# Window attention and two MLPs on one core: dilated rows in 1 KB runs, and a new order for the start

## The chip, the core and the metric

The kernel runs on one core of one Trainium2 chip. The core has five engines that run side by side, each with an instruction queue that it works through strictly in order: TensorE (PE, matmuls and transposes into PSUM), VectorE (DVE), ScalarE (ACT), GpSimd (POOL) and SyncE (SP, which here only issues DMAs). An instruction waits on semaphores until its inputs are there, and whatever stands behind it on the same engine waits with it. The metric is device time in microseconds. Before the change, three runs took 951.55, 952.68 and 952.71 us (median 952.68).

## The reference

Three stages in a row, all in float32:

```
attention   q, k, v of 4 batches x 8 heads x 576 positions x 64
            heads 0-3: each position sees itself and the 31 before it
            heads 4-7: itself and 31 more, every 4th position back (dilation 4)
            softmax over those, times v
x           the attention output as 2304 tokens x 512
MLP 1       h = x @ w_in1 (512 x 2048);  g = max(0.01 h, h);   y = g @ w_out1
MLP 2       h = y @ w_in2;  g = max(h,0) + log1p(exp(-|h|));   out = g @ w_out2
```

The weights come as 64-bit floats. They are read as pairs of 32-bit words and put together on the chip.

## The kernel before

**Stages.** The 2304 tokens are cut into eight blocks (`w` = 0 to 7) of 288, half a batch each. A block's attention is done in four pairs of heads (`p` = 0 to 3; pairs 0 and 1 are plain, 2 and 3 dilated). Below, pairs 0 to 3 are those of block 0 and pairs 4 to 7 those of block 1. MLP 1 runs in slots: for one block and one of 16 chunks of 128 hidden units, `g1` (12 matmuls on L586, 128x128 by 288 columns) makes the hidden values in PSUM, ACT and DVE split them into a high and a low half (`gh`, `gl`), and `g2` (12 matmuls on L620) adds to the output two slots later. Each product is done three times, high by high, high by low, low by high, so that fp32r matmuls give float32 precision. Slots 0 to 3 are block 0 with weight chunks 0 to 3, slots 4 to 7 block 1 with the same chunks, slots 8 to 11 block 0 with chunks 4 to 7, and so on. MLP 2 follows in blocks of 384 tokens. From about 130 us on TensorE is fed without a break, so the order of work matters in the start alone.

**The early blocks.** Blocks 0 and 1 (`early`) have their own way through attention. `load_rows` loads the rows of q or k of four heads (one plain or one dilated group) into a tile `rows`; `pe_trans` (L402) transposes them on TensorE, two heads at a time; `evac_k`, `evac_q` (L417, L420) copy them from PSUM to SBUF on ACT; `scores_early` (L451 the mask, L455 the products) makes the scores; `scores_copy` copies one half of them to SBUF on ACT (L469) and one on DVE (L471); `rowmax` (L506) takes the maximum on POOL; `less_max` (L510, DVE) and `exp` (L513, ACT) follow; `pv` (L526), `inv` (L536 to L538, DVE), `xT` (L549), `x_hi` (L562, ACT) and `x_lo` (L566, DVE) make the block's x in two halves. The first `g1` of a block needs all four pairs.

The dilated rows are loaded so that token 4p+i stands in partition p, place i, with the four heads side by side. A run of consecutive bytes is then one token of one head, 64 numbers or 256 B, and one DMA is issued for each i:

```
t = wraw.tile([n // nb, nb, 4, D], F32, tag="raw", name="rows", bufs=NRAW)
rs = src[self.b, self.h0:self.h0 + 4, lo:self.s0 + T1, :].rearrange("h (p i) d -> i p h d", i=nb)
for i in range(nb):
    eng.dma_start(out=t[:, i], in_=rs[i])
```

Block 0's q rows are issued by ACT, all other DMAs by SP.

**Weights.** Each of 32 pieces of MLP 1 (piece 2f for chunk f of w_in, 2f+1 for w_out) is loaded (L221, L225) and converted in a chain: ACT `cf` (L232), DVE `cp` (L236), DVE join (L240), ACT low word (L245), add (L249), ACT high half `w` (L269), low half (L274). The add and the low half of pieces 0 to 5 run on DVE, those of pieces 6 to 21 on POOL. POOL holds one library at a time: the maxima need one, the adds and low halves another, and the adds wait (`order=early`) until all eight maxima of blocks 0 and 1 are done, so that the library is changed once there. The first piece on POOL, number 6, is the w_in of chunk 3, which slot 3 needs.

**Late blocks.** Blocks 2 to 7 use other buffers (`kt`, `qz`, `v`), which POOL clears once in the start (`late_clear`, L317).

**The order.** Nothing is in a fixed order: every step is an `Op` with an engine, an assumed cost, what it depends on and a due time. `run_schedule` plays the program through with those costs, lets each engine take the ready step that is due first, and emits the instructions in that order. `COLD` multiplies the assumed TensorE costs of block 0, `lag` is the assumed time from an issued DMA to its use, `TL` the due time of the clears, `TR` that of block 1's maxima relative to slot 0. A changed cost can so reorder every engine.

Of the kernel before, what the change touches and what calls it, by code (L numbers as in the profile page):

```python
# [22 lines left out]
def kernel(  # L23
# [75 lines left out]
    def run_schedule(slots):  # L99
# [226 lines left out]
    class Pair:  # L326
# [25 lines left out]
        def load_rows(self, which, eng):  # L352
# [4 lines left out]
            t = wraw.tile([n // nb, nb, 4, D], F32, tag="raw", name="rows", bufs=NRAW)  # L357
            rs = src[self.b, self.h0:self.h0 + 4, lo:self.s0 + T1, :].rearrange("h (p i) d -> i p h d", i=nb)
            for i in range(nb):
                eng.dma_start(out=t[:, i], in_=rs[i])  # L360
# [35 lines left out]
        def pe_trans(self, which):  # L396
            src = rows[self.w, self.dil, which]
            pp, nb = src.shape[0], src.shape[1]
            o = 2 * (self.p % 2)
            ps = ps_y.tile([P, nb, pp], F32, tag=f"y{o + which}", name="tr")  # L400
            for i in range(nb):
                nc.tensor.transpose(  # L402
                    out=ps[:, i], in_=src[:, i, o:o + 2, :].rearrange("p h d -> p (h d)"), identity=ident[0:pp, 0:pp])
# [62 lines left out]
        def scores_copy(self, j):  # L466
            o = self.s[:, :, j]
            if j == 0:
                nc.scalar.activation(out=o, in_=self.sc[j], func=AF.Copy)  # L469
            else:  # L470
                nc.vector.tensor_copy(out=o, in_=self.sc[j])  # L471
# [275 lines left out]
    COLD = 1.6  # L747
    TL, TR = 30.0, -12.0
# [29 lines left out]
    for t, to in [(t, 0.0) for t in kt_b + qz_b] + [(t, 1.0) for t in v_b]:  # L778
        late_clear.append(Op("pool", 0.7, clear, nc.gpsimd, t, to, order=late_clear[-1:], target=TL))
    for w in range(NW):  # L780
        first_slot = min(s for s in range(NS1) if order[s][0] == w)
        for p in range(NPAIR):
# [14 lines left out]
            if early:  # L797
                if p % 2 == 0:
                    ls = []
                    for which in (1, 0):  # L800
                        qd = "dma" if which or w else "act"
                        nb = 4 if dil or w and which else 3
                        o = Op(qd, 0.48 * nb, a.load_rows, which, nc.scalar if qd == "act" else nc.sync, acq=["raw"],
# [3 lines left out]
                        ls.append(Op("bw", 1.1 if w == 0 else 1.4, lambda: None, deps=[o], **m))  # L807
                    early_rows[w, dil] = ls
                lk, a.lq = early_rows[w, dil]
            else:  # L810
                lk = Op("dma", 1.95, a.load_k, order=[prev(1, "lq")], acq=["kr"], **m)
                a.lq = Op("dma", 1.95, a.load_q, order=[lk], acq=["qr"], **m)
# [256 lines left out]
```

## Time and profile before

| | us |
|---|---|
| median of three runs | 952.68 |
| the profiled execution, whole time | 952.19 |
| its span, first to last instruction | 950.3 |
| TensorE busy | 926.1 (97% of the span) |
| VectorE busy | 665.2 (70%) |
| ScalarE busy | 469.4 (49%) |
| GpSimd busy | 162.6 (17%) |

1.9 us of the profiled execution lie outside its span. The shares are means over the whole; the change touches the first 100 us, and there each stretch has another limit. Of the last chain, 89% of the span is TensorE and 6% VectorE, and the VectorE part lies almost wholly before 130 us.

### The profile page before, as it was taken

Reading aid. Unit: us, or ns where it says so; the run is one execution under the profiler, and the core shown is the slowest. Engines: PE = TensorE matmul, PEld = TensorE weight load, DVE = VectorE, ACT = ScalarE, POOL = GpSimd, SP = SyncE. Lnnn points to the kernel's source line nnn. Section 1 sums busy time; section 2 is a strip of 40 time slices with the busy share of each in tenths; the row PEclk is TensorE's granted clock in tenths of the full one; section 3 lists DMA queues with packets and bytes.
Section 4 is the critical chain, followed back from the end, with each engine's and each line's share of the span. In section 5 each row is a group of like instructions: output and inputs, shape, how many; then the busy total and the mean of one; then the engine's idle time right before and its main releaser. Section 6 shows DMA issues by size and latency. Waiting matters only on the chain.

```text
span 950.3 us, 15906 instructions
## 1 busy us (share of the span) xinstructions
PE 926.1 (97%) x6002; PEld 876.8 (92%) x6002; DVE 665.2 (70%) x1313; ACT 469.4 (49%) x973; POOL 162.6 (17%) x114
## 2 busy tenths in 40 slices
PE   7989899999999999999999999999999999999997
PEld 6788799999999999999999989899899899899896
DVE  6678899667466674665744487777877877877775
ACT  4566675344344443444446654644644645544543
POOL 4537731011010110200208710000000000000000
PEclk9999899999999999999999999999999999999999
DMA  9968001546264444453257410200200000000000
GB/s 216 256 192 277 10 1 29 142 118 155 93 151 109 142 105 131 123 122 119 76 175 239 136 35 1 66 1 1 67 1 1 34 1 1 34 1 1 34 1 33
DMA packets 137552, 81.52 MB, mean 86 GB/s; under 512 B 101380, under 2 KB 121860, under 8 KB 137476
## 3 DMA queue, kind: packets, MB, share of 16 engines
q1 hardware_dynamic: 135076, 79.92, 29.8%
q10 hardware_dynamic: 2400, 0.59, 0.4%
q8 instruction: 47, 0.77, 0.3%
q14 instruction: 29, 0.24, 0.1%
HBM read 62.65 MB, written 17.83 MB: 85 GB/s over the span
## 4 chain that ended last, share of the span: by engine, by line
PE 89%; DVE 6%; ACT 1%; DMA 1%; issue 1%; POOL 0%; SPq 0%; DVEq 0%; ACTq 0%
PE h L586 40%; PE yo L720 20%; PE yp L620 19%; PE pv L526 4%; PE sc L482 2%; DVE cf L240 2%; DVE cp L236 1%; PE sc L455 1%; PE xt L549 1%; DVE gl L607 1%; DMA rows<-in_k_dram 1%; PE tr L402 1%; PE sc L451 0%; DMA raw<-in_moe_w_out_dram 0%; ACT cf L232 0%
## 5 line engine op out<-in xcount | busy, mean ns | idle before, releaser
L586 PE MATMUL h<-xh,w 128*128 128x288 f32 (+1 forms) x1792 | 447.6, 319 | 1.8 <-POOL w L274 1.8
L586 PEld LDWEIGHTS h<-xh,w 128*128 128x128 f32 x1792 | 316.4, 191 | 6.3 <-POOL w L274 2.1
L586 PE MATMUL h<-xl,w 128*128 128x288 f32 (+1 forms) x896 | 283.7, 317 | 0.1
L620 PE MATMUL yp<-gh,w 128*128 128x288 f32 x1024 | 232.4, 301 | 7.3 <-DVE ys L634 3.6
L620 PEld LDWEIGHTS yp<-gh,w 128*128 128x128 f32 x1024 | 173.5, 189 | 8.9 <-DVE ys L634 4.3
L720 PE MATMUL yo<-w,gh 128*128 128x512 f32 x576 | 180.3, 394 | 0.3 <-ACT gh L703 0.3
L586 PEld LDWEIGHTS h<-xl,w 128*128 128x128 f32 x896 | 170.8, 191 | 4.6 <-DVE xl L566 0.3
L620 PE MATMUL yp<-gl,w 128*128 128x288 f32 x512 | 152.3, 297 | 0.0
L607 DVE TENSOR_TENSOR gl<-hc,gh 128x288 fp32r<-128x288 f32 x128 | 74.0, 578 | 94.5 <-ACT gh L603 93.3
L676 ACT ACTIVATE ex<-h 128x384 f32<-128x384 f32 x96 | 47.2, 491 | 174.5 <-PE h L586 174.5
L720 PEld LDWEIGHTS yo<-w,gh 128*128 128x128 f32 x576 | 106.9, 188 | 18.3 <-ACT gh L703 1.2
L720 PE MATMUL yo<-w,gl 128*128 128x512 f32 x288 | 114.4, 397 | 0.2 <-DVE gl L707 0.2
L603 ACT ACTIVATE gh<-hc 128x288 fp32r<-128x288 f32 x128 | 56.7, 443 | 88.3 <-PE yp L620 87.5
L598 ACT ACTIVATE hc<-h 128x288 f32<-128x288 f32 x128 | 52.2, 408 | 94.7 <-PE h L586 90.9
L506 POOL PARTITION_ALL_REDUCE mx<-s x24 | 48.0, 2001 | 296.2 <-DVE s L496 288.2
L620 PEld LDWEIGHTS yp<-gl,w 128*128 128x128 f32 x512 | 96.9, 189 | 0.0
L687 DVE TENSOR_SCALAR z<-ex 128x384 f32<-128x384 f32 x96 | 35.5, 370 | 77.2 <-ACT ex L677 77.2
L720 PEld LDWEIGHTS yo<-w,gl 128*128 128x128 f32 x288 | 54.1, 188 | 13.7 <-DVE gl L707 1.3
L694 DVE TENSOR_TENSOR ln<-ln,ex 128x384 f32<-128x384 f32 x96 | 54.5, 568 | 3.2
L707 DVE TENSOR_TENSOR gl<-ln,gh 128x384 fp32r<-128x384 f32 x96 | 53.6, 558 | 3.6 <-ACT gh L703 1.6
L696 DVE SCALAR_TENSOR_TENSOR ln<-h,ln 128x384 f32<-128x384 f32 x96 | 53.5, 558 | 3.2
L690 DVE TENSOR_TENSOR z<-ex,z 128x384 f32<-128x384 f32 x96 | 53.6, 558 | 3.0
(73 smaller groups left out, 1062.3 us busy)
## 6 DMA issues: line engine op xcount, KB each, us to landing
raw<-in_moe_w_in_dram SPq DMA_DIRECT2D x32, 512.0 KB
raw<-in_moe_w_out_dram SPq DMA_DIRECT2D x32, 512.0 KB
w<-cf SPq DMA_DIRECT2D x32, 256.0 KB
w<-w SPq DMA_DIRECT2D x32, 256.0 KB
y<-ys SPq DMA_DIRECT2D x8, 576.0 KB
out_dram<-o SPq DMA_DIRECT2D x18, 256.0 KB
qr<-in_q_dram SPq DMA_DIRECT2D x96, 36.0 KB
yr<-y SPq DMA_DIRECT2D x4, 576.0 KB
```

The costliest lines, as they stand in the source:

```text
L506: nc.gpsimd.partition_all_reduce(self.mx, self.sf, channels=P, reduce_op=bass_isa.ReduceOp.max)
L586: nc.tensor.matmul(out=h, lhsT=a[:, c, :], rhs=b_[:, c, :], start=(c == 0 and a is whi and b_ is xh), stop=(c == NC - 1 and a is wlo))
L598: nc.scalar.activation(out=hc, in_=hbank.pop(s), func=AF.Prelu, alpha=0.01)
L603: nc.scalar.activation(out=gh, in_=hcopy[s], func=AF.Copy)
L607: eng.tensor_sub(out=gl, in0=hcopy.pop(s), in1=gparts[s][0].bitcast(F32))
L620: nc.tensor.matmul(out=ybank[e], lhsT=a[:, e * P:(e + 1) * P], rhs=b_, start=(first and a is whi and b_ is gh), stop=(last and a is wlo))
L676: nc.scalar.activation(out=ex, in_=hbank[NS1 + s], func=AF.Abs)
L690: nc.vector.tensor_sub(out=z, in0=ex, in1=z)
L694: nc.vector.tensor_tensor(out=ln, in0=ln, in1=ex, op=ALU.min)
L696: nc.vector.scalar_tensor_tensor(out=ln, in0=hbank.pop(NS1 + s), scalar=0.0, in1=ln, op0=ALU.max, op1=ALU.add)
L707: nc.vector.tensor_sub(out=gl, in0=soft.pop(s)[1], in1=gh.bitcast(F32))
L720: nc.tensor.matmul(out=obank[c, t], lhsT=a[:, t * P:(t + 1) * P], rhs=b_, start=(f == 0 and a is gh and b_ is whi), stop=(f == NF - 1 and ...
```

## The change

Four things. The dilated rows of blocks 0 and 1 are loaded by one DMA each, with the four tokens of a partition in one run of 4 x 64 numbers (1 KB). Two heads no longer stand side by side, so a transpose takes two neighbouring residues (tokens 4p+2u and 4p+2u+1) of one head: the 64-row halves of `kt`, `qt` are then residues, no longer heads, the number of transposes and matmuls is the same, and `scores_copy` puts the pieces back in the old order with a strided output. The transfer time of row loads and other loads is modelled apart from the issue (`landing`), with other costs. Due times change: `COLD` 1.6 to 1.2, `TL` from a due time of 30 to an earliest time of 36, `TR` -12 to -2. And with these the order changes on every engine.

```
         def load_rows(self, which, eng):
...
+            if self.dil:
+                t = wraw.tile([n // nb, 4, nb, D], F32, tag="raw", name="rows", bufs=NRAW)
+                eng.dma_start(
+                    out=t.rearrange("p h i d -> p h (i d)"),
+                    in_=rs.rearrange("h (p i) d -> p h (i d)", i=nb))
+            else:
...
         def pe_trans(self, which):
...
+            if self.dil:
+                cols = [src[:, o + j, 2 * u:2 * u + 2, :] for j in range(2) for u in range(2)]
+            else:
+                cols = [src[:, i, o:o + 2, :] for i in range(src.shape[1])]
...
         def scores_copy(self, j):
-            o = self.s[:, :, j]
+            if self.dil:
+                o = self.s[:, j::2]
+                i = self.sc[j].rearrange("x (h u) m -> x u h m", h=2)
+            else:
+                o, i = self.s[:, :, j], self.sc[j]
...
-                return 2.0
+                return 1.5
...
-    COLD = 1.6
-    TL, TR = 30.0, -12.0
+    COLD = 1.2
+    TL, TR = 36.0, -2.0
...
-        late_clear.append(Op("pool", 0.7, clear, nc.gpsimd, t, to, order=late_clear[-1:], target=TL))
+        late_clear.append(Op("pool", 0.7, clear, nc.gpsimd, t, to, order=late_clear[-1:], start=TL))
...
+    def landing(op, us, m):
+        return Op("bw", us, lambda: None, deps=[op], **m)
...
-                        o = Op(qd, 0.48 * nb, a.load_rows, ...
+                        o = Op(qd, 0.75 if dil else 0.65 * nb, a.load_rows, ...
-                        ls.append(Op("bw", 1.1 if w == 0 else 1.4, lambda: None, deps=[o], **m))
+                        ls.append(landing(o, 1.3 if dil else 0.47 * nb, m))
...
-                lk = Op("dma", 1.95, a.load_k, order=[prev(1, "lq")], acq=["kr"], **m)
-                a.lq = Op("dma", 1.95, a.load_q, order=[lk], acq=["qr"], **m)
+                o = Op("dma", 1.95, a.load_k, order=[prev(1, "i_lq")], acq=["kr"], **m)
+                lk = landing(o, 1.0, m)
+                a.i_lq = Op("dma", 1.95, a.load_q, order=[o], acq=["qr"], **m)
+                a.lq = landing(a.i_lq, 0.9, m)
```

On SP the change takes 3 + 3 + 3 issues away (three dilated loads of four DMAs each become one), on ACT 3. The sixth weight piece, which stood behind block 1's v and dilated rows, now stands right behind the first five, and block 0's dilated v ahead of block 1's dilated rows.

At the very start TensorE had twelve transposes of plain rows, then four of dilated rows, then the scores of pairs 0 and 1, then twelve more dilated transposes. Now the scores of pairs 0 and 1 follow the twelve plain transposes, and all sixteen dilated ones come after them.

The second place is TensorE ahead of the first product of MLP 1 (`h`). In the rows 96 is a plain pair and 72 a dilated one (and `tr` 104 the k rows of a dilated pair of block 1). Before: the second half of `pv` of pair 2, `xt` of pair 1, `pv` of pair 3, `xt` 2, `pv` 4, `xt` 3, `pv` 5, `xt` 4, first `h`:

```order
L526 MATMUL pv<-ev,es 72x65 x4
L549 MATMUL xt<-ident,xn 128x96 x3
L526 MATMUL pv<-ev,es 72x65 x8
L549 MATMUL xt<-ident,xn 128x72 x4
L526 MATMUL pv<-ev,es 96x65 x6
L549 MATMUL xt<-ident,xn 128x72 x4
L526 MATMUL pv<-ev,es 96x65 x6
L549 MATMUL xt<-ident,xn 128x96 x3
L586 MATMUL h<-xh,w_313 128x288
```

Now: the second half of `pv` of pair 3, `xt` 2, a transpose of pair 7's k, `pv` 4, the scores of pair 7 (the mask matmuls and `ekq`), `xt` 3, first `h`:

```order
L543 MATMUL pv<-ev,es 72x65 x4
L566 MATMUL xt<-ident,xn 128x72 x4
L414 MATMUL tr<-ident,rows 128x104 x4
L543 MATMUL pv<-ev,es 96x65 x6
L464 LDWEIGHTS identb
L464 MATMUL sc<-masksb,identb 128x288
L464 LDWEIGHTS identb
L464 MATMUL sc<-masksb,identb 128x288
L468 MATMUL sc<-ekq 128x72 x8
L566 MATMUL xt<-ident,xn 128x72 x4
L603 MATMUL h<-xh,w_378 128x288
```

`pv` 5 and `xt` 4 of block 1 moved behind the first `h`, and the scores of pairs 6 and 7 moved nearer to it.

On DVE the copies of the scores of pairs 6 and 7 (`es_106`, `es_107`) stood early, around the low half of the second w_in chunk:

```order
L566 TENSOR_TENSOR xl_451<-xt_452,xh_450 128x288
L471 COPY es_106<-sc_474 128x288
L274 TENSOR_TENSOR w0_495<-cf_287,w0_495 128x512
L471 COPY es_107<-sc_499 128x288
L236 TENSOR_SCALAR cp_425<-cf_424 128x512
```

Now they stand behind the low half of x of pair 3 (`xl_369<-xt_566`), the last that the first `h` needs:

```order
L583 TENSOR_TENSOR xl_369<-xt_566,xh_368 128x288
L553 TENSOR_SCALAR rd_583<-pv_537 96x6
L554 RECIPROCAL rd_583<-rd_583 96x6
L555 TENSOR_TENSOR xn_536<-pv_537,rd_583 96x384
L527 TENSOR_TENSOR es_105<-es_105,emx_113 128x576
L236 TENSOR_SCALAR cp_562<-cf_561 128x512
L488 COPY es_106<-sc_481 128x2x2x72
L274 TENSOR_TENSOR w0_579<-cf_411,w0_579 128x512
L249 ISA cf_423<-cf_423,cp_424 128x1024
L240 SCALAR_TENSOR_TENSOR cf_561<-cf_561,cp_562 128x512
L583 TENSOR_TENSOR xl_609<-xt_610,xh_608 128x288
L488 COPY es_107<-sc_549 128x2x2x72
```

Both copies moved behind some twenty instructions of weights and normalisation.

On POOL all seven clears stood between the eight maxima (`emx`), and the change of library (`ISA` alone) and the first add and low half came right after the last maximum:

```order
L317 MEMSET qz_89 128x576
L317 MEMSET qz_90 128x576
L317 MEMSET v_93 128x520
L506 ISA emx<-es 128x576
L317 MEMSET v_94 128x520
L317 MEMSET v_95 128x520
L506 ISA emx<-es 128x576
L249 ISA
L249 TENSOR_TENSOR cf<-cf,cp 128x512
L274 TENSOR_TENSOR w_775<-cf,w_775 128x512
```

Now four of the clears come after the change of library, two of them between the first add and the first low half:

```order
L317 MEMSET qz_89 128x576
L523 ISA emx<-es 128x576
L249 ISA
L249 TENSOR_TENSOR cf<-cf,cp 128x512
L317 MEMSET qz_90 128x576
L317 MEMSET v_93 128x520
L274 TENSOR_TENSOR w_765<-cf,w_765 128x512
L249 TENSOR_TENSOR cf<-cf,cp 128x512
L317 MEMSET v_94 128x520
L317 MEMSET v_95 128x520
L274 TENSOR_TENSOR w_831<-cf,w_831 128x512
```

The first low half on POOL (w_775 before, w_765 now) is that of slot 3 in both.

## Rows read from the trace of the kernel before

**Rows 1.** Busy time by stretch: PE, PEld, DVE, ACT, POOL, PEclk, DMA share, GB/s
```profile
70.00:130.00 60.00, 52.59 (x347) 50.76 (x345) 52.06 (x65) 38.20 (x80) 40.49 (x29) 0.91 0.39 122
130.00:950.00 820.00, 814.37 (x5256) 773.84 (x5256) 565.69 (x1146) 394.32 (x821) 91.67 (x56) 1.00 0.25 72
```

**Rows 2.** The chain that ended last, 70 to 130 us, shares by line
```profile
by line: DVE cf L240 25.5%; DVE cp L236 21.8%; DVE gl L607 13.9%; issue 11.2%; PE yp L620 4.2%; PE h L586 3.5%; DVE ys L630 3.1%; ACT cf L232 2.9%; DVE w L274 2.8%; ACT gh L603 2.8%; DVE qz L437 2.4%; ACT hc L598 1.4%; DVE ys L634 1.3%; ACT
```

**Rows 3.** TensorE in order of time: start, length, instruction [idle before <- releaser]
```profile
5.53 2.10 PE L402 MATMUL tr<-ident,rows 96*128 96x96 f32 x12 [0.69 <-DMA rows<-in_k_dram]
...
9.28 0.69 PE L451 MATMUL sc<-masksb,identb 128*128 128x288 bf16 x2
...
42.27 2.15 PE L526 MATMUL pv<-ev,es 104*72 104x65 f32 x16 [1.46 <-issue]
44.67 0.71 PE L549 MATMUL xt<-ident,xn 72*128 72x72 f32 x4 [0.26 <-DVE rd L536]
...
48.95 2.15 PE L526 MATMUL pv<-ev,es 128*96 128x65 f32 x12 [0.78 <-DVE xn L538]
...
51.28 0.59 PE L586 MATMUL h<-xh,w 128*128 128x288 f32 x1
...
64.60 0.85 PE L586 MATMUL h<-xh,w 128*128 128x288 f32 x2 [1.85 <-POOL w L274]
```

**Rows 4.** ScalarE's queue in order of time, its first DMA issues
```profile
0.75 5.53 ACTq L360 DMA_DIRECT2D rows<-in_q_dram  x7
```

**Rows 5.** GpSimd in order of time, columns as in Rows 3
```profile
8.72 0.38 POOL L321 PARTITION_ALL_REDUCE warm<-ident  x1 [6.00 <-issue]
...
39.49 1.07 POOL L317 MEMSET v<- 128x520 f32 x2
43.96 2.39 POOL L506 PARTITION_ALL_REDUCE emx<-es  x1 [3.40 <-DVE rd L536]
53.78 1.76 POOL L249 TENSOR_TENSOR cf<-cf,cp 128x512 uint32<-128x512 uint32 x1 [7.43 <-DMA kr<-in_k_dram]
62.24 2.30 POOL L274 TENSOR_TENSOR w<-cf,w 128x512 fp32r<-128x512 f32 x1 [6.70 <-ACT w L269]
...
68.89 1.64 POOL L274 TENSOR_TENSOR w<-cf,w 128x512 fp32r<-128x512 f32 x1 [1.23 <-ACT w L269]
71.01 1.28 POOL L249 TENSOR_TENSOR cf<-cf,cp 128x512 uint32<-128x512 uint32 x1 [0.48 <-DMA raw<-in_moe_w_out_dram]
```

**Rows 6.** VectorE in order of time, up to 65 us, columns as in Rows 3
```profile
39.25 0.46 DVE L471 COPY es<-sc 128x288 f32<-128x288 f32 x1 [1.46 <-PE sc L455]
39.63 1.21 DVE L236 TENSOR_SCALAR cp<-cf 128x512 uint32<-128x512 uint32 x1
...
47.72 0.16 DVE L536 TENSOR_SCALAR rd<-pv 96x6 f32<-96x6 f32 x1 [1.15 <-PE pv L526]
...
48.61 0.68 DVE L249 CUSTOM_DVE_ANT_0 cf<-cf,cp 128x1024 uint16<-128x1024 uint16 x1
49.21 0.45 DVE L566 TENSOR_TENSOR xl<-xt,xh 128x288 fp32r<-128x288 f32 x1
49.58 0.68 DVE L240 SCALAR_TENSOR_TENSOR cf<-cf,cp 128x512 uint32<-128x512 uint32 x1
50.17 0.68 DVE L274 TENSOR_TENSOR w<-cf,w 128x512 fp32r<-128x512 f32 x1
...
53.31 0.41 DVE L236 TENSOR_SCALAR cp<-cf 128x512 uint32<-128x512 uint32 x1
53.64 0.75 DVE L510 TENSOR_TENSOR es<-es,emx 128x576 f32<-128x576 f32 x1
```

**Rows 7.** VectorE in order of time, from 70 us on, columns as in Rows 3
```profile
70.10 0.74 DVE L607 TENSOR_TENSOR gl<-hc,gh 128x288 fp32r<-128x288 f32 x1 [0.72 <-ACT gh L603]
70.77 0.45 DVE L566 TENSOR_TENSOR xl<-xt,xh 128x288 fp32r<-128x288 f32 x1
...
74.80 0.41 DVE L236 TENSOR_SCALAR cp<-cf 128x512 uint32<-128x512 uint32 x1
```

More of the change, by code (lines that the diff above doesn't have):

```diff
@@ L356, in load_rows @@
             nb = DIL if self.dil or n % 3 else 3
[L357 to L360, printed above, removed]
+            rs = src[self.b, self.h0:self.h0 + 4, lo:self.s0 + T1, :]
+            if self.dil:
[4 more added lines that the diff above has]
+            else:
+                t = wraw.tile([n // nb, nb, 4, D], F32, tag="raw", name="rows", bufs=NRAW)
+                rs = rs.rearrange("h (p i) d -> i p h d", i=nb)
+                for i in range(nb):
+                    eng.dma_start(out=t[:, i], in_=rs[i])
             rows[self.w, self.dil, which] = t
@@ L397, in pe_trans @@
             src = rows[self.w, self.dil, which]
-            pp, nb = src.shape[0], src.shape[1]
+            pp = src.shape[0]
             o = 2 * (self.p % 2)
-            ps = ps_y.tile([P, nb, pp], F32, tag=f"y{o + which}", name="tr")
-            for i in range(nb):
+            if self.dil:
+                cols = [src[:, o + j, 2 * u:2 * u + 2, :] for j in range(2) for u in range(2)]
+            else:
+                cols = [src[:, i, o:o + 2, :] for i in range(src.shape[1])]
+            ps = ps_y.tile([P, len(cols), pp], F32, tag=f"y{o + which}", name="tr")
+            for i, c in enumerate(cols):
                 nc.tensor.transpose(
-                    out=ps[:, i], in_=src[:, i, o:o + 2, :].rearrange("p h d -> p (h d)"), identity=ident[0:pp, 0:pp])
+                    out=ps[:, i], in_=c.rearrange("p a d -> p (a d)"), identity=ident[0:pp, 0:pp])
             if not self.dil:
@@ L466, in scores_copy @@
         def scores_copy(self, j):
-            o = self.s[:, :, j]
+            if self.dil:
[3 more added lines that the diff above has]
+                o, i = self.s[:, :, j], self.sc[j]
             if j == 0:
-                nc.scalar.activation(out=o, in_=self.sc[j], func=AF.Copy)
+                nc.scalar.activation(out=o, in_=i, func=AF.Copy)
             else:
-                nc.vector.tensor_copy(out=o, in_=self.sc[j])
+                nc.vector.tensor_copy(out=o, in_=i)
         def scores(self, half):
@@ L801 @@
                         qd = "dma" if which or w else "act"
-                        nb = 4 if dil or w and which else 3
-                        o = Op(qd, 0.48 * nb, a.load_rows, which, nc.scalar if qd == "act" else nc.sync, acq=["raw"],
+                        nb = 4 if w and which else 3
+                        o = Op(qd, 0.75 if dil else 0.65 * nb, a.load_rows, which, nc.scalar if qd == "act" else nc.sync, acq=["raw"],
                                order=[o for o in row_loads if o.earlier < w], **m)
```

6 lines of the change are left out of this document (4 added, 2 removed).

## The prediction

> **What bounds the kernel now.** I read the busy time by stretch first. From 130 us to the end TensorE is busy 814 of 820 us [rows 1], and the change alters nothing there, so all that can be won or lost lies before. In 70 to 130 us no engine is full, TensorE 52.6 and VectorE 52.1 of 60 us, but the chain of waits in that stretch runs through VectorE's weight lines: cf, cp, gl, ys, w and qz make 70.8% of it, matmuls 8% [rows 1, 2]. TensorE idles 7.4 us there (60 less 52.6), which is the room that a gain has. Then TensorE in order of time, for what it waits on before the first product of MLP 1. It starts the scores at 9.28, waits 1.46, 0.26 and 0.78 us further on, starts the first h at 51.28, and in slot 3 it stands 1.85 us until GpSimd has the low half of the weight, at 64.60 [rows 3]. Last GpSimd: its last maximum runs 43.96 to 46.35, then 7.43 us pass to the first add (the change of library), and the first low half comes at 62.24 [rows 5]. That low half is the gate through which slot 3 and all later slots must go.
>
> **The start.** The plain transposes begin at 5.53, when their last rows land. Of the twelve in that row ten are plain (two stand in rows ahead of it, two of the twelve are dilated), so they end at 5.53 + 10/12 x 2.10 = 7.28 [rows 3]. ACT, which copies them out, is busy issuing seven DMAs from 0.75 to 6.28 [rows 4]. With four it is done at about 0.75 + 4/7 x 5.53 = 3.9, so the copies follow the transposes, and the last q copy that the scores need ends near 7.6 (an estimate: 7.28 and one copy of 0.35). The scores start at 7.6 for 9.28, 1.7 us earlier. The four dilated transposes that stood before them come back later, at 2.10/12 = 0.175 each, 0.7 us. They cannot wait for data: they now stand behind two pairs of scores, at about 12 us, and their rows have landed by 9.28 even as it is, since the scores stood behind them. Lead: 1.0 us. How much faster 1 KB runs land does not matter by this, since it ends before it is needed; if it also let the plain rows land sooner, up to another 1 us, it would show in the first transposes.
>
> **To the first h.** The three waits of 1.46, 0.26 and 0.78 lie between 40 and 49 us. In the new order other work stands there (transposes and scores of pairs 6 and 7), so I take them as gone: 2.5 us. pv of pair 5 (2.15) and xt of pair 4 (about 0.5, the row's 0.71 less the overlap with its neighbour) move behind the first h: 2.65 us. Lead there: 1.0 + 2.5 + 2.65 = 6.2 us, the first h at about 45.1. The cost of the moved work is not saved, it only comes later.
>
> **What is late next: GpSimd's library.** The last maximum needs the copies of pair 7's scores. On VectorE these now stand behind the low x of pair 3, which waits for xt of pair 3, the last TensorE work before the first h. So: 45.1, ACT's high half 0.4, low half 0.45 [rows 6], gives 46.0. Behind it on VectorE in order: the three instructions of a normalisation 0.89 (47.72 to 48.61), less_max 0.75, cp 0.41, copy of pair 6 0.46, low half of a weight 0.68, add 0.68, join 0.68, low x 0.45, copy of pair 7 0.46 [rows 6]: 5.5 us. Beside GpSimd's own work one of them is stretched, as the cp at 39.63 was next to a clear, 1.21 for 0.41 [rows 5, 6]: 0.8. The copy ends at 51.5 to 52.3, and with 2.39 for the maximum [rows 5] it ends at 53.9 to 54.7, I take 54.1, against 46.35 before: 7.8 us later, although TensorE is 6 us ahead.
>
> From there to the gate: change of library 7.43 (the nearest row, the same change in the same place; the lower bound is the 6.00 ahead of the very first maximum), add 1.28 to 1.76, I take 1.5, two clears 1.07 (the pair at 39.49), low half 1.64 to 2.30, I take 1.8 [rows 5]. 54.1 + 7.43 + 1.5 + 1.07 + 1.8 = 65.9. Before, the low half ended at 62.24 + 2.30 = 64.54. The gate opens 1.4 us later than before, between -0.6 (53.9 + 6.00 + 1.28 + 1.07 + 1.64 = 63.9) and +2.7 (54.7 + 7.43 + 1.76 + 1.07 + 2.30 = 67.3). The lead of 6 us is then lost as one wait of TensorE in slot 3, some 6 to 8 us long.
>
> [...]
>
> **Behind the gate.** What was done before it is the gain. Before, gl of slot 3 stood at 70.10, and VectorE then had to do the low x of pair 7, a cp, two transposes of q and a join, 70.77 to 74.80, 4.0 us [rows 7]. In the new order these five stand ahead of the gl of slot 3, in time in which VectorE waits for TensorE anyway. From the gate to that gl it took 70.10 - 64.60 = 5.5 us, so gl is now at 71.4, 1.3 later, with 4.0 us more behind it: VectorE is 2.7 ahead. TensorE ends slot 3 1.3 later, but xt of pair 6 (0.5) is done, so it reaches slot 4 0.8 later. GpSimd: the second add starts at 65.9 and ends at 67.4, two clears to 68.5, so the second low half starts at 68.5 for 68.89 [rows 5]: 0.4 ahead. Since the chain of 70 to 130 us is VectorE's to 0.71 [rows 2], I weigh the three so: 0.71 x 2.7 and 0.29 x -0.2 (the mean of the other two) make 1.86 us, and I take off 0.1 for the strided copies (four on each engine; the trace shows none, the plain copy is 0.46 [rows 6], and I bound the change at -0.05 to +0.1 each). Gain 1.8 us.
>
> Nothing else is on the path. Nine fewer issues free SP (at 5.53/7 = 0.8 us each, if they go as on ACT [rows 4]), but the DMA queue behind it is what limits the loads, and weights of chunks 7 and up wait for pair 7 in both orders. Later clears on GpSimd can cost VectorE something: the one seen beside a clear was stretched by 0.8 us; four clears, at most 3.2 us, at least nothing. They lie in the 7 us in which TensorE waits, two of them at least, so I count none.
>
> [...]
>
> **Sum.** Profiled execution 952.19 - 1.8 = 950.4 us. That execution lies 0.5 us under the median of 952.68, which I take as spread. A difference under 0.2%, 1.9 us, is about what a measurement cannot tell from no change.
>
> **Rivals.**
> Fast gate. The change of library takes 6.00 as at 8.72, and the add and low half are not stretched [rows 5]: the gate opens at 54.1 + 6.00 + 1.28 + 1.07 + 1.64 = 64.1, 1.8 us earlier than I take, and all behind it. For it: each of the three was seen. Against: 7.43 in the very place. 950.4 - 1.8 = 948.6. If VectorE's stretch were also 2 us shorter, 946.6.
> Slower: late last maximum. VectorE's ten rows in front of pair 7's copy, and that copy, take longer than the 5.5 + 0.8 us that I allow, because more than one of them is stretched by 0.8 beside GpSimd's maximum and clears. Each microsecond there is one at the gate, with TensorE idle. It decides from 1.8 us on: a last maximum that ends after 55.9 makes the kernel slower than before. With six rows stretched instead of one, 4.0 us more: 954.4. For it: the cp at 39.63 [rows 6]. Against: from 47.72 to 50.85 seven such rows ran back to back, but while GpSimd stood still.
> No use of the lead. VectorE's 4.0 us ahead are waited away, since cp and join also need ACT and GpSimd, and the end of the start is set by GpSimd's sixteen pieces, which are level. Then 951.8, no change. For it: GpSimd is busy 40.5 of 60 us with its waits on the same chain [rows 1].
>
> **Chances.** Forecast 0.42 (its own range 949.0 to 951.8), fast gate 0.22, late maximum 0.22, no use 0.14. Faster by over 0.2%: half of the first and all of the second, 0.43. Slower by over 0.2%: most of the third, 0.18. The rest 0.39. The range takes in both outer cases but for their ends: 947.0 to 954.6.
>
> **What would show it.** Scores starting near 7.6 and first h near 45; the last maximum ending near 54; one long TensorE wait in slot 3 released by GpSimd's low half, near 65.9; gl of slot 3 near 71 with the q transposes behind it. A last maximum before 50, or no long wait in slot 3, would make me wrong towards faster; a gate after 67.5 towards slower. If the chain of 70 to 130 us were no longer VectorE's, the weight of its lead would be wrong.

## The result, and the profile after

The changed kernel takes 958.70 us (median of four runs, 957.46 to 960.96) against 952.32 for the kernel before: ratio 1.0074, 95% interval 1.0062 to 1.0086. It is slower; forecast were 950.4 and a range of 947.0 to 954.6. The profiled execution took 958.49 us, 6.3 more than the one before.

TensorE in order of time, the rows that answer to [rows 3]:

```profile
5.98 1.86 PE L414 MATMUL tr<-ident,rows 96*128 96x96 f32 x10 [1.19 <-DMA rows<-in_k_dram]
7.63 0.69 PE L464 MATMUL sc<-masksb,identb 128*128 128x288 bf16 x2
...
20.00 4.00 PE L414 MATMUL tr<-ident,rows 80*128 80x80 f32 x14 [1.00 <-DMA rows<-in_k_dram]
...
47.30 0.59 PE L603 MATMUL h<-xh,w 128*128 128x288 f32 x1
...
62.20 2.42 PE L543 MATMUL pv<-ev,es 104*72 104x65 f32 x16 [3.83 <-DVE xn L555]
66.07 0.71 PE L566 MATMUL xt<-ident,xn 72*128 72x72 f32 x4 [1.45 <-DVE xn L555]
69.63 0.61 PE L603 MATMUL h<-xh,w 128*128 128x288 f32 x1 [2.85 <-ACT w L269]
71.19 0.85 PE L603 MATMUL h<-xh,w 128*128 128x288 f32 x2 [0.71 <-POOL w L274]
```

The scores start 1.65 us sooner and the first h 4.0. At 20 us the transposes of block 1 wait for rows that a weight piece stands ahead of. From 58 us on TensorE waits four times, and its last wait ends at 71.19, where it ended at 64.60. GpSimd, answering to [rows 5]:

```profile
11.81 0.38 POOL L321 PARTITION_ALL_REDUCE warm<-ident  x1 [9.08 <-issue]
...
39.31 1.96 POOL L523 PARTITION_ALL_REDUCE emx<-es  x1 [6.82 <-DVE es L488]
41.15 0.94 POOL L317 MEMSET kt<- 128x440 f32 x2
50.93 3.43 POOL L523 PARTITION_ALL_REDUCE emx<-es  x1 [8.85 <-ACT es L530]
54.24 0.65 POOL L317 MEMSET qz<- 128x576 f32 x1
54.79 4.43 POOL L523 PARTITION_ALL_REDUCE emx<-es  x1
67.66 1.25 POOL L249 TENSOR_TENSOR cf<-cf,cp 128x512 uint32<-128x512 uint32 x1 [8.45 <-issue]
...
69.87 1.26 POOL L274 TENSOR_TENSOR w<-cf,w 128x512 fp32r<-128x512 f32 x1
```

The last maximum ends at 54.79 + 4.43 = 59.22 for 46.35. The first add starts at 67.66 for 53.78, the first low half ends at 71.13 for 64.54. VectorE's copies that the two last maxima need, answering to [rows 6]:

```profile
48.03 0.46 DVE L583 TENSOR_TENSOR xl<-xt,xh 128x288 fp32r<-128x288 f32 x1 [2.85 <-ACT xh L579]
...
50.29 0.45 DVE L488 COPY es<-sc 128x288 f32<-128x288 f32 x1
...
52.83 0.44 DVE L488 COPY es<-sc 128x288 f32<-128x288 f32 x1
```

They stand behind the low x of pair 3 at 48.03, as the order said. Busy time by stretch (columns as in [rows 1]):

```profile
70.00:130.00 60.00, 53.83 (x364) 51.80 (x364) 50.57 (x68) 39.39 (x82) 41.67 (x31) 0.93 0.41 118
130.00:950.00 820.00, 815.15 (x5265) 774.64 (x5264) 570.41 (x1149) 395.66 (x824) 95.51 (x59) 1.00 0.25 71
```

By busy time the two kernels look alike from 70 us on. The chain that ended last, 70 to 130 us, by line (answers to [rows 2]):

```profile
by line: DVE cf L240 16.9%; issue 15.8%; DVE cp L236 13.5%; DVE gl L624 11.9%; DMA v<-in_v_dram 9.3%; POOL cf L249 6.1%; POOL w L274 5.7%; ACT w L269 2.8%; DVE ys L647 2.4%; ACT cp L245 2.4%; ACT gh L620 2.0%; DVE ys L651 1.9%; POOL v L317 
```

VectorE's lines make 46.6% of it in place of 70.8; GpSimd's weight lines and a DMA have come in. Where the time goes is seen better by the slot. Each of the 128 slots of MLP 1 has one high half of h on ScalarE (L603 before, L620 after); its start, less that of the same slot in the profiled run of before, is the lag. It is worked out so for every profiled run of this study (us, minus is ahead). A line is of one run, and this can lie at the edge of its kernel's: those of e1, e6, e8 and e16 are of runs 1.3 to 2.9 us under their medians, those of e4, e7, e9, e10, e12 and e13 of runs 1.0 to 2.0 us over them.

```
slot                                   0     3     8    20    82   127
after                               -2.7  +7.7  +3.2  +4.8  +5.6  +6.2
e1  copies early                    -3.3  +1.2  -2.9   0.0  +1.6  +2.0
e2  rows only, on before            +0.7  +0.7  +0.8  +0.7  +0.7  +0.9
e3  sixth piece back                -4.8  +2.7  -1.8  +2.4  +3.3  +6.6
e4  piece 6 on VectorE              -3.2  +4.6  +0.4  +3.5  +4.8  +7.9
e5  old order from first add        -3.9  +5.8  +5.8  +5.8  +5.9  +5.5
e6  e1 and e5                       -2.7  -0.3  -0.3  -0.3  -0.1   0.0
e7  before, new order from there    +0.4  +3.9  -1.5  +1.6  +3.8  +4.2
e8  e1, old order from slot 24      -2.9  +1.1  -3.4  -0.3  -0.3  -0.8
e9  due time back                   +0.9  +8.2  +3.7  +7.6  +7.6  +8.7
e10 e9, old order from slot 24      -0.2  +7.2  +2.6  +6.5  +6.7  +7.1
e11 e8, rows and clears forward     -4.3  -0.9  -4.7  -1.6  -1.5  -1.7
e12 e10 with more                   -1.4  +3.8  -0.8  +3.3  +3.4  +2.9
e13 before, late maxima             -1.4  +3.4  +2.4  +4.0  +4.1  +3.6
e14 e10, buffer freed               -0.2  +6.4  +1.9  +4.4  +4.4  +3.9
e15 e11, old order from slot 9      -4.3   0.0  -3.8  -3.2  -3.2  -3.3
e16 e11, old order from slot 14     -5.5  -1.1  -6.4  -3.0  -2.8  -3.3
```

The first line tells what has to be explained: 2.7 us ahead at slot 0, 7.7 late at slot 3, 4.5 of that made good by slot 8, and then 3.0 us lost again, 1.6 by slot 20 and 1.4 after it.

### The profile page after: what moved, and what is told of

The parts are those of the page before. It is cut to its first block, busy times and chain, and to the rows that moved or that the text cites. A ratio compares the mean times of both kernels' runs of the same rounds, so it can differ in the third digit from the quotient of the medians.

```text
span 956.4 us, 15897 instructions
## 1 busy us (share of the span) xinstructions
PE 925.8 (97%) x6002; PEld 875.0 (91%) x6002; DVE 662.8 (69%) x1313; ACT 469.2 (49%) x973; POOL 163.3 (17%) x114
## 4 chain that ended last, share of the span: by engine, by line
PE 85%; DVE 5%; DMA 3%; POOL 2%; issue 2%; ACT 2%; SPq 0%; DVEq 0%; ACTq 0%; POOLq 0%
PE h L603 39%; PE yo L737 20%; PE yp L637 18%; PE pv L543 4%; PE sc L499 2%; DMA raw<-in_moe_w_out_dram 1%; DVE cf L240 1%; DMA rows<-in_k_dram 1%; DVE cp L236 1%; DVE gl L624 1%; PE xt L566 1%; PE sc L468 1%; POOL emx L523 1%; POOL w L274 1%; DMA v<-in_v_dram 1%
## 5 line engine op out<-in xcount | busy, mean ns | idle before, releaser
L603 PE MATMUL h<-xh,w 128*128 128x288 f32 (+1 forms) x1792 | 446.5, 318 | 3.6 <-ACT w L269 2.8
L603 PEld LDWEIGHTS h<-xh,w 128*128 128x128 f32 x1792 | 315.2, 190 | 8.3 <-ACT w L269 3.1
L603 PE MATMUL h<-xl,w 128*128 128x288 f32 (+1 forms) x896 | 283.0, 316 | 0.0
L637 PE MATMUL yp<-gh,w 128*128 128x288 f32 x1024 | 231.1, 300 | 7.4 <-ACT gh L620 3.0
L637 PEld LDWEIGHTS yp<-gh,w 128*128 128x128 f32 x1024 | 172.6, 189 | 8.7 <-ACT gh L620 3.2
L603 PEld LDWEIGHTS h<-xl,w 128*128 128x128 f32 x896 | 170.2, 190 | 4.3
L637 PE MATMUL yp<-gl,w 128*128 128x288 f32 x512 | 152.2, 297 | 1.0 <-DVE gl L624 1.0
L637 PEld LDWEIGHTS yp<-gl,w 128*128 128x128 f32 x512 | 96.7, 189 | 1.7 <-DVE gl L624 1.5
L620 ACT ACTIVATE gh<-hc 128x288 fp32r<-128x288 f32 x128 | 56.5, 441 | 84.9 <-PE yp L637 84.3
L737 PEld LDWEIGHTS yo<-w,gl 128*128 128x128 f32 x288 | 54.1, 188 | 13.7 <-DVE gl L724 1.3
```

The source lines that it names most:

```text
L603: nc.tensor.matmul(out=h, lhsT=a[:, c, :], rhs=b_[:, c, :], start=(c == 0 and a is whi and b_ is xh), stop=(c == NC - 1 and a is wlo))
L620: nc.scalar.activation(out=gh, in_=hcopy[s], func=AF.Copy)
L637: nc.tensor.matmul(out=ybank[e], lhsT=a[:, e * P:(e + 1) * P], rhs=b_, start=(first and a is whi and b_ is gh), stop=(last and a is wlo))
L737: nc.tensor.matmul(out=obank[c, t], lhsT=a[:, t * P:(t + 1) * P], rhs=b_, start=(f == 0 and a is gh and b_ is whi), stop=(f == NF - 1 and ...
```

## The experiments

**e1. The copies of pairs 6 and 7 ahead of the low x of pair 3.** `find` picks operations of the written-out order, `place` moves one.

```diff
+    place(find("scores_copy", n=6, a0=1)[0], find("scores_copy", n=5, a0=1)[0])
+    place(find("scores_copy", n=7, a0=1)[0], find("x_lo", n=3)[0], after=False)
+    place(find("less_max", n=5)[0], find("scores_copy", n=7, a0=1)[0], after=False)
```

> The changed kernel, with three VectorE instructions moved forward: the score copies of pairs 6 and 7 and less_max of pair 5 stand ahead of the low x of pair 3. Gate theory (the kernel's time follows the first low half on GpSimd, which ends at 71.1 in the changed kernel and 64.5 before): the last maximum ends near 49.8 instead of 59.2, the change of library near 58, the first low half near 61 to 63, and the time falls from 958.5 to 949 to 951. Rival, the loads (block 1's rows land late behind the sixth weight piece) or the data layout make the loss: these are as in the changed kernel, so at most 1 us comes back, 957 or more.

Measured: 957.19 us (ratio 1.0054, 1.0038 to 1.0071), its runs in two groups, 954.1 and 954.3, and 957.0 to 958.5; the traced one is the 954.3. The last maximum ends at 49.49 and slot 3 is 1.2 late instead of 7.7, so the chain that I blamed was cut. The first low half ends at 64.13, later than expected, after a wait of 0.85 us for ScalarE. And the time came back only in part: 1.5 us by the medians, the number of the rival. Slot 8 is 2.9 ahead and slot 127 2.0 late. A second loss stands behind the first.

**e2. The rows alone.** The order of before on all engines, with the 1 KB rows, their transposes and the strided copies of the change.

```diff
+            if self.dil:
+                t = wraw.tile([n // nb, 4, nb, D], F32, tag="raw", name="rows", bufs=NRAW)
...
+                o = self.s[:, j::2]
+                i = self.sc[j].rearrange("x (h u) m -> x u h m", h=2)
```

> The kernel before in its own order on all engines, with the 1 KB row loads, the transposes by residue and the strided copies alone. Gate theory: the order is that of before, so the last maximum stays near 46 and the first low half near 64.5; the dilated rows land 1 to 2 us sooner, which may bring up to 1.5 us: 950.5 to 952.5. Rival, the layout makes the loss (strided copies, transposes, loads): 955 or more.

Measured: 953.67 us (1.0016, 1.0005 to 1.0026), above what was expected. The new layout costs some 1.5 us (0.5 to 2.5) and gains nothing by itself. In the old order it brings no lead at the start; the new order without the layout was not run.

**e3. The sixth weight piece behind block 1's rows.**

```diff
+    place(find("load", layer=0, f=2, which=1)[0], find("load_rows", w=1, dil=True, a0=0)[0])
```

> The changed kernel with the load of the sixth weight piece moved back behind block 1's dilated rows. In the changed kernel TensorE loses 2.7 us at 19 to 24 us waiting for block 1's rows. Gate theory: the rows land about 1.4 to 2.7 us sooner, the first product, the last maximum and the first low half all come that much sooner, 955.8 to 957.1. Rival, the loads alone make the loss: 952 to 953. Rival, the wait is hidden by a later one: 958 to 959.

Measured: 958.53 us (1.0069, 1.0049 to 1.0089), no change against after, the number of the last rival, though the wait at 20 us went and slot 3 came 5.0 us sooner. The lead was lost twice: 4.2 us from slot 8 to 20, and 3.3 between slots 82 and 127. In the second lies one wait of 2.2 us, the only one that TensorE has from 400 to 415 us, behind this chain (start, length, what):

```profile
402.09 0.41 SPq L399
402.50 0.05 issue
402.55 0.02 SPq L399
...
403.11 0.42 SPq L258
403.52 0.05 issue
403.57 5.22 DMA raw<-in_moe_w_out_dram
...
408.88 0.67 ACT cf L232
...
409.57 0.43 DVE cp L236
410.00 0.68 DVE s L527
...
410.70 0.69 ACT s L530
...
411.44 0.73 PE pv L543 x8
```

A weight piece is issued at 403.57 behind the v rows on SP. ScalarE's and VectorE's first operations on it stand in their queues ahead of the softmax of a pair, so the pair waits for the weight, and TensorE for the pair: `PE pv L543 <- ACT s L530: 2.2, 1, 2.2`. From 410 to 415 us (columns as in [rows 1]) TensorE is then busy 3.56 of 5 us at a granted clock of 0.73:

```profile
410.00:415.00 5.00, 3.56 (x23) 3.56 (x24) 3.36 (x8) 1.62 (x4) 0.00 (x0) 0.73 0.62 187
```

In before the same piece was issued at 400.69 and was there at 404.65; TensorE waited 0.2 us. In e4 the same wait is 3.1 us, in after 0.8, in e1 0.2. That it also parts the two groups of e1's runs is likely and not shown.

**e4. Slot 3 without GpSimd's library.** The add and low half of its weight on VectorE.

```diff
+    for name in ("add", "split_lo"):
+        find(name, layer=0, f=3, which=0)[0].args = (nc.vector,)
```

> The changed kernel with the add and the low half of weight piece 6 on VectorE instead of GpSimd, at their places in the order, so that slot 3 no longer waits for the change of library; piece 7 is then the first behind it, needed two slots later. Gate theory: slot 3 starts near 67 instead of 71 and GpSimd has one piece less, 954 to 956. Rival, VectorE's own work is what binds from 60 us on: its two more instructions cost 1.4 us, 959 to 960.

Measured: 958.25 us (1.0071, 1.0055 to 1.0088). Neither forecast came. Slot 3 is 3.1 us sooner than in after and slot 8 almost level with before, yet the end is as late. This made the order behind the gate the suspect, since the order differs from before at 377 of the 1190 places of VectorE's plan, from the start nearly to the end of MLP 1.

**e5. The order of before from GpSimd's first add on.** All planned operations from there on, on all engines, in the order of the kernel before, as far as data and buffers allow.

```diff
+    schedule = other_order_from(find("add", layer=0, f=3, which=0)[0])
```

> The changed kernel with the order of all engines put back to that of before from the first add of GpSimd (chunk 3) on; what is ahead of it (the start, block 0, the maxima, the clears) stays as changed. By the theory that the order behind the gate costs some 3.0 us of its own (in the changed kernel's trace the high halves of h run 3.2 us late at slot 8 and 6.2 at slot 127): 955 to 956 us, 3.2 at slot 8 kept to the end. By the rival that the lateness of the gate alone makes the whole loss and the order behind it is worth nothing: 958 to 959. By the rival that the start's loss sits in DMAs that this doesn't move: 958 to 959 too, with slot 8 late as before.

**e6.** The three moves of e1, then that of e5.

```diff
+    place(find("scores_copy", n=6, a0=1)[0], find("scores_copy", n=5, a0=1)[0])
...
+    schedule = other_order_from(find("add", layer=0, f=3, which=0)[0])
```

> As the last, and with VectorE's copies of pairs 6 and 7 taken ahead as in the first experiment, so that the gate is in time. By the theory that two causes add (late gate 4 to 6 us, order behind it 3 to 5): slot 8 is 2.9 us ahead of the kernel before and stays so: 949 to 950 us, faster than before. By the rival that the lead is given back by VectorE's and ScalarE's own load, whatever the order: 952 to 954.

**e7.** The line of e5 in the kernel before, with the order of after as the other.

> The mirror: the kernel before up to GpSimd's first add, from there on the order of the changed kernel on all engines. By the theory that this order costs 3 to 5 us by itself: 955 to 957 us against 952.3, with the high halves of h on time up to slot 8 and some 3 late from slot 16 to 20 on. By the rival that the order is harmless and only the late gate spoils it: 952 to 953.

**e8.** As e6, with the cut later:

```diff
+    schedule = other_order_from([o for o in schedule if o.fn is g1_hi and o.args == (24,)][0])
```

> The first experiment (copies of pairs 6 and 7 ahead) with the order of before only from slot 24 on, at some 150 us. The hole at 85 to 140 us stays, the later ones go (0.0 at slot 24 and +2.0 at slot 127 in the first experiment's trace, and at 405 us a wait of 2.2 us and a lower clock in one other trace). By the theory that the later part of the order costs 1 to 5 us, not in every run: 952 to 953 and runs close together. By the rival that only the part up to slot 24 matters: 954 to 957.5 as in the first experiment.

Measured (before 952.05): e5 957.29 (1.0054, 1.0040 to 1.0068), e6 953.50 (1.0019, 1.0010 to 1.0028), e7 955.15 (1.0030, 1.0019 to 1.0042), e8 952.48 (1.0003, 0.9994 to 1.0012). e7 and e8 came as expected, e5 and e6 did not. What follows:

Under the order of before the late last maximum costs 3.8 us (e5 less e6, which differ in the three moves of e1 alone), for 1.5 under that of the change (after less e1), and in e5 the lag is set at slot 3 and hardly moves after it (+5.8 at slots 3, 8 and 20). The new order behind the gate costs 3.1 us by itself (e7 less before). It has two faces: in e7's line it loses 3.5 us up to slot 3 (GpSimd's first low half waits 9.89 us for ScalarE's high half of the same weight) and makes good 5.4 up to slot 8; between 8 and 20 it loses 3.1, and after that 2.6 more. e8 has none of the last part: from slot 20 on its lag goes from -0.3 to -0.8. My 955 to 956 for e5 was too little since I took the 3.2 of after's slot 8, where the new order had already made up some. My 949 to 950 for e6 was wrong: its lead of 2.7 at slot 0 is gone at slot 3. GpSimd was ready in time, but its first low half waited 2.12 us for ScalarE and ended at 64.18, for 64.54 in before:

```profile
62.59 1.59 POOL L274 TENSOR_TENSOR w<-cf,w 128x512 fp32r<-128x512 f32 x1 [2.12 <-ACT w L269]
```

So a lead at the start buys nothing when the gate does not open sooner.

**e9 and e10. One number of the planner.** The maxima of block 1 due 10 us sooner, as in before; e10 with the cut of e8.

```diff
-    TL, TR = 36.0, -2.0
+    TL, TR = 36.0, -12.0
```

> The changed kernel with one number of the planner put back: the maxima of block 1 are due 10 us sooner again (TR from -2 to -12). VectorE's copies of pairs 6 and 7 then stand ahead of the low x of pair 3 by the planner itself. By the theory that this number made the last maxima late: the last maximum ends by 49.5 us instead of 59.2, slot 3 at most 1.2 late, and the time as in the first experiment, 953 to 957, since the order behind is not that of before either. By the rival that the late maxima come from the long maxima beside VectorE (3.4 and 4.4 us) and not from the order: the last maximum ends after 55, 957 to 959.

> As the last, with the order of before from slot 24 on. By the theory of two causes that add: 951.5 to 952.5, no faster than before, as the lead of the start is spent at the gate. By the rival that only one of the two matters: equal to the last.

Measured (before 952.55): e9 958.58 (1.0078, 1.0063 to 1.0092), e10 957.72 (1.0065, 1.0052 to 1.0078). Wrong, and instructive. In e9 the copies came at 38.23 and 40.75, twelve us sooner, but the last maximum ran as late as in after, as the rival had it, and for another reason:

```profile
38.89 2.23 POOL L523 PARTITION_ALL_REDUCE emx<-es  x1 [6.88 <-DVE es L488]
...
55.32 3.80 POOL L523 PARTITION_ALL_REDUCE emx<-es  x1 [12.87 <-DVE es L527]
...
67.06 2.25 POOL L249 TENSOR_TENSOR cf<-cf,cp 128x512 uint32<-128x512 uint32 x1 [6.96 <-ACT cf L232]
```

It waited for L527, the subtraction of pair 5's maximum, at 54.40 on VectorE, which frees one of the two buffers of the maxima (e14 tries this).

**e11.** e8, with the sixth piece as in e3 and all late clears ahead of the maximum of pair 6.

```diff
+    place(find("load", layer=0, f=2, which=1)[0], find("load_rows", w=1, dil=True, a0=0)[0])
+    clears = [o for o in late_clear if schedule.index(o) > schedule.index(find("rowmax", n=6)[0])]
+    for o in clears:
+        place(o, find("rowmax", n=6)[0], after=False)
```

> Copies of pairs 6 and 7 ahead, the order of before from slot 24 on, and two more edits: the sixth weight piece behind block 1's dilated rows, and all late clears ahead of the maximum of pair 6. If what holds slot 3 is the chain last copy, last maximum, library, add, clears, low half, then the rows bring the copies of pair 7 some 2 us forward and the clears leave 1.1 us of the chain: slot 3 at 68 us instead of 70.7, and 950 to 951.5. By the rival that VectorE's and ScalarE's conversions hold it: 952.5 as without the two.

**e12.** e10 with these lines and those of e4.

> One planner number back, order of before from slot 24 on, sixth piece behind block 1's rows, clears ahead of pair 6's maximum, and the add and low half of piece 6 on VectorE, so that slot 3 waits for no library. If the library holds the start, slot 3 comes 3 us sooner and the time is 949 to 951; by the rival that VectorE has no room for two more operations there: 952 to 954.

Measured: e11 950.18 us (0.9983, 0.9972 to 0.9993), e12 953.59 (1.0019, 1.0009 to 1.0028). e11 is the first that beats the kernel before, and 2.3 us better than e8: with the rows in time and the clears out of the way the first low half ends at 63.15, and slot 3 is 0.9 ahead. Which of the two moves did it was not parted. e12 missed its forecast and came in the range of its rival; its maximum again waits for L527, until 53.05.

**e13. The late maxima alone, in the kernel before.**

```diff
+    place(find("scores_copy", n=6, a0=1)[0], find("x_lo", n=4)[0])
+    place(find("scores_copy", n=7, a0=1)[0], find("scores_copy", n=6, a0=1)[0])
+    place(find("rowmax", n=6)[0], find("scores_copy", n=6, a0=1)[0])
+    place(find("rowmax", n=7)[0], find("scores_copy", n=7, a0=1)[0])
```

> The kernel before with one thing of the change alone: VectorE's copies of pairs 6 and 7, and with them the two last maxima, stand behind the low x of pair 4 (52.5 us in before). The last maximum then ends at some 57.5 instead of 46.4; with the library's 7.4, the add and the low half of 1.3 and 2.3, the first low half ends at 69 instead of 64.5. By the theory of the late gate: slot 3 is 4 to 5 late and stays so, 956 to 957.5. By the rival that the loss is made by the new order and the gate only shows it: 952 to 953.

**e14.** e10 with pair 5's subtraction moved.

```diff
+    place(find("less_max", n=5)[0], find("scores_copy", n=7, a0=1)[0])
```

> The kernel with one planner number back and the order of before from slot 24 on, and one operation of VectorE moved: the subtraction of pair 5's maximum, which stood at 54.4 us and frees the buffer of the last maximum, goes right behind the copy of pair 7. If that buffer held the last maximum, it ends at 43 to 49 instead of 58, slot 3 comes at 69 to 71 instead of 76.8, and the time is 951.5 to 953 instead of 957.7. By the rival that VectorE's own load held the gate there: 956 to 958.

**e15 and e16.** e11 with the cut at slot 9, and at slot 14, instead of 24.

> The fastest kernel so far with the order of before from slot 9 on instead of slot 24. It is 4.7 us ahead at slot 8 and 1.6 at slot 20. If those 3 us belong to the order between the slots, the lead of 4.7 stays: 947 to 948.5. If they are conversions put off by slots 3 to 8, which have to be made up: 950 to 951.5.

> As the last, with the order of before from slot 14 on (the hole of 3.0 us in which the PE waits for the high half of h lies there, 5.7 us ahead at slot 13 and 1.9 at slot 14). If that hole is the order's own: 947 to 949. If it is put off work: 950 to 951.5.

Measured (before 952.06): e13 954.78 us (1.0028, 1.0018 to 1.0039), e14 956.62 (1.0045, 1.0032 to 1.0057), e15 948.30 (0.9957, 0.9944 to 0.9969), e16 950.36 (0.9983, 0.9974 to 0.9992).

e13 shows the mechanism alone on GpSimd:

```profile
52.37 4.12 POOL L506 PARTITION_ALL_REDUCE emx<-es  x2 [18.29 <-DVE es L471]
63.55 1.37 POOL L249 TENSOR_TENSOR cf<-cf,cp 128x512 uint32<-128x512 uint32 x1 [7.06 <-issue]
65.66 1.27 POOL L274 TENSOR_TENSOR w<-cf,w 128x512 fp32r<-128x512 f32 x1 [0.74 <-ACT w L269]
```

The first add comes 9.8 us later than in [rows 5], at 63.55, and slot 8 is 2.4 late, less than the 4 to 5 that I expected at slot 3; in e5 it comes at 67.08, and slot 8 is 5.8 late. Both give the same point, 63.55 - 2.4 = 61.2 and 67.08 - 5.8 = 61.3: up to a first add at some 61.2 the lateness is free, and from there on each microsecond is one. [rows 5] shows why: in before the first low half waited 6.70 us for ScalarE's high half (`6.70 <-ACT w L269`), so GpSimd had that much time to spare. Under the order of before the end of the first low half, less the 64.54 of before, is the lag of slot 8 to 0.1 us: 2.4 in e13, 5.8 in e5 (69.07 + 1.27), -0.4 in e6. Behind slot 8 e13 loses 1.6 more, by slot 20, though its order there is that of before; its traced run is the slowest of eight, and this was not followed.

In e14 the last maximum ended at 43.42, so the buffer had held it. But the gate stayed shut for another reason:

```profile
57.61 2.12 POOL L249 TENSOR_TENSOR cf<-cf,cp 128x512 uint32<-128x512 uint32 x1 [13.21 <-ACT cp L245]
...
67.23 2.47 POOL L274 TENSOR_TENSOR w<-cf,w 128x512 fp32r<-128x512 f32 x1 [5.99 <-ACT w L269]
```

GpSimd was ready and the low half waited 5.99 us for ScalarE's high half of the same weight. The add ended at 59.73, but in ScalarE's queue this high half, at 66.53, stands behind two exponentials and a conversion of another weight that wait for VectorE (0.97, 0.36 and 0.67 us); the first and the last of them:

```profile
61.45 0.68 ACT L530 ACTIVATE es<-es 128x576 f32<-128x576 f32 x1 [0.97 <-DVE es L527]
...
65.96 0.66 ACT L232 ACTIVATE cf<-raw 128x512 f32<-128x512 f32 x1 [0.67 <-DVE w L274]
66.53 0.61 ACT L269 ACTIVATE w<-cf 128x512 fp32r<-128x512 f32 x1
```

So two chains end at the same gate, and taking one away from e10 gave 1.1 us of the 5 that I expected.

e15 and e16 differ in the order between slots 9 and 14 alone, and no run of the one reaches into those of the other: this order costs 2.1 us. With that of before from slot 9 on the lag goes from -3.8 at slot 8 to -3.2 and stays, so what e11 loses there (3.1 by slot 20) is for the most part not work put off. e16 missed: its 950.36 is that of e11, in the range that I gave for work put off. Its trace is of its fastest run, and so level with e15's.

The hole, TensorE's wait of 3.0 us for the high half of h, I had in the wrong place. At slot 14, where e11's lag jumps from -5.7 to -1.9, ScalarE is late with a half that TensorE does not need yet; TensorE waits 0.36 us there, for VectorE. The longest wait of 82 to 145 us in after, e1, e8, e11 and e14 (`PE yp L637 <- ACT gh L620: 3.0, 1, 3.0`) is for the high half of slot 17. In after:

```profile
131.73 0.39 ACT L615 ACTIVATE hc<-h 128x288 f32<-128x288 f32 x1
132.32 0.66 ACT L232 ACTIVATE cf<-raw 128x512 f32<-128x512 f32 x1 [0.20 <-POOL w L274]
133.76 0.67 ACT L232 ACTIVATE cf<-raw 128x512 f32<-128x512 f32 x1 [0.78 <-POOL w L274]
134.34 0.42 ACT L620 ACTIVATE gh<-hc 128x288 fp32r<-128x288 f32 x1
...
134.80 0.37 PE L637 MATMUL yp<-gh,w 128*128 128x288 f32 x1 [3.01 <-ACT gh L620]
```

The high half is ready to run at 132.1 and stands behind two weight operations that wait for GpSimd. This wait is not there in before, e13, e15 and e16. But e16, without it, is no faster than e11, so it is not shown to make the loss; in which waits the 2.1 us go stays open.

e15 is 3.8 us faster than the kernel before, and 10.4 by the medians faster than the changed one.

## Why the prediction was wrong

**The start.** Right in number: scores at 7.63 for the 7.6 worked out. That was luck in part, as two errors cancel: the ten transposes started at 5.98 and not at 5.53, and the mask matmuls, with which the scores begin, followed them at once and did not wait for the q copies as I had it (these ran from 7.40 to 8.29). Wrong by 2.2 us at the first h (47.30 for 45.1): I counted no loss for block 1's rows, which wait behind the sixth weight piece; e3 takes that wait away and has the first h at 45.19.

**The last maximum.** This step failed. That it would be late, because the copies stand behind the low x of pair 3, was right. The size was not: 59.22 for 54.1, 5.1 us. The copy of pair 7 ended at 53.27 where 51.7 stood behind the sum, 1.6: the low x of pair 3 ended 2.5 late, mostly by the late first h, and VectorE's rows behind it took 4.8 for 5.7, with none stretched. I left out the maximum of pair 6, which GpSimd must do first: with its clear it held the last one from 53.27 to 54.79, 1.5. And the last maximum took 4.43 for 2.39, 2.0.

**The library and the gate.** 8.45 for 7.43, 1.0 later; add, clears and low half 3.47 for 4.37, 0.9 sooner. The gate opened at 71.13 instead of 65.9, 5.2 us late. In e1 to e3, e5 to e11, e13, e15 and e16 the change of library took 6.73 to 7.76. The idle time ahead of the very first maximum, which was my lower bound, does not hold still either: it is 6.00 in before and 9.08 in after.

**Behind the gate.** The gate was 6.6 us later than in before and slot 8 only 3.2, so work done ahead was worth 3.4; the forecast had 1.4 + 1.8 = 3.2. In ten other kernels with the new order up to slot 8 (e1, e3, e7 to e11, e14 to e16) it was worth 2.5 to 3.9. Right for that stretch, though by another road: the two transposes of q and the low x of pair 7 do stand ahead of the gl of slot 3, as in the order, but this gl runs at 77.95, 6.8 us behind the gate, where I had 5.5 [rows 7], and VectorE no longer rules the chain [rows 2].

```profile
76.59 0.45 DVE L583 TENSOR_TENSOR xl<-xt,xh 128x288 fp32r<-128x288 f32 x1
76.96 0.96 DVE L449 STREAM_TRANSPOSE qz<-qr 64x288 f32<-64x288 f32 x2
77.95 0.52 DVE L624 TENSOR_TENSOR gl<-hc,gh 128x288 fp32r<-128x288 f32 x1
```

This step failed too: the change alters nothing from 130 us on, the order matters in the start alone, nothing else is on the path. The order differs nearly to the end of MLP 1, and it lost 3.0 us between slots 8 and 127. e7 and e8 show that this is the order; e15 beside e16 puts some 2 us of such a loss into slots 9 to 13, and the chain of e3 shows one place behind slot 82.

e3 is closest to the kernel that I forecast: first h at 45.19 (45.1), the last maximum's end at 54.72 (54.1), the gate at 66.16 (65.9), and slot 8 1.8 us ahead, the very gain that I had.

```profile
45.19 0.59 PE L603 MATMUL h<-xh,w 128*128 128x288 f32 x1
...
52.68 2.04 POOL L523 PARTITION_ALL_REDUCE emx<-es  x1
...
64.89 1.27 POOL L274 TENSOR_TENSOR w<-cf,w 128x512 fp32r<-128x512 f32 x1
```

Yet it takes 958.53 us. With the gate nearly where the forecast had it, what is lost behind slot 8 alone makes the forecast wrong by 8 us.

**Sum.** Forecast -1.8, result +6.3, 8.1 apart: 5.2 at the gate and 3.0 behind it make 8.2. This adds up for the traced run of after; e3 shows that the two do not simply add, since there the first is 0.3 and the second 8.4.

**The rivals.** The slower one happened in its effect (a last maximum after 55.9, TensorE idle in slot 3) but not by the cause that it gave: it held VectorE's rows to be what stretches, and these ran at their usual lengths; the late first h, the maximum of pair 6 and the stretched maxima made it. Its price, 954.4, was too small also since nothing was charged for the order behind. The point from which it decides lay lower than I said, a first add at 61.2 instead of 63.3 (55.9 + 7.43). The fast gate did not come. Where the last maximum was early, in e6 and e15, the gate still opened at 64.18 and 64.06 only, since GpSimd then waited 2.12 and 4.78 us for ScalarE's high half. No use of the lead, 951.8, did not come either: what was done ahead was worth its 3.4 us at slot 8, and losses behind took it.

## What to carry to other kernels

Where a change lets a planner write the whole order anew, compare the order to its end on each engine, not only where the diff aims, and follow the lag by work item, since busy shares hide it. Before a lead at the start is counted, name every chain that ends at the first gate behind it, with each operation of the engine there in its order: here a buffer, a copy, a maximum, the library and ScalarE's half took turns. And an operation that waits for another engine should not stand in front of one that TensorE waits for.

## What was not expected of the hardware

The same maximum over partitions took 1.96 us at 39.31 and 3.43 and 4.43 at 50.93 and 54.79, beside VectorE's back to back work on weights; in e13, beside the normalisation of a pair, two took 4.12 together, and VectorE's subtraction at their end (L510, at 54.57) 1.71 for its usual 0.75. VectorE's shift of a weight (cp) took 0.42 alone, 1.24 at 57.23 in after, but 0.42 at 55.26 beside the same maximum. GpSimd's lengths are rough in this profile. Whether the two engines hold each other up there, and which of them stretches when, was not tried by itself.

TensorE's granted clock stood at 0.57 in 60 to 70 us of after, with TensorE busy 3.48 us and waits of 3.83, 1.45 and 2.85 us ending there (columns as in [rows 1]):

```profile
60.00:70.00 10.00, 3.48 (x21) 2.98 (x22) 5.71 (x17) 3.59 (x7) 2.34 (x4) 0.57 0.98 337
```

In before it stood there at 0.83:

```profile
60.00:70.00 10.00, 7.63 (x56) 7.19 (x55) 7.38 (x20) 5.87 (x13) 5.17 (x3) 0.83 0.91 306
```

In after it was 0.50 from 62 to 74 us, 0.73 from 74 to 76 and 1.00 from 76 to 78. The last wait ended at 71.19, and behind it a matmul of h with the low x took 0.44 us at 72.55 for 0.30 at 76.80. So part of what these waits cost came after them. It was not so behind every wait: in e4, with its wait of 3.1 us, the clock is 1.00 in 410 to 415 us and in 415 to 420.
